# Threshold attention and a feed-forward part: one slot per head against one slot per pair of heads

## The chip, the cores and the metric

The kernel runs on one core of one Trainium2 chip. The metric is the device time of one execution in microseconds (us). Before the change the median of three runs is 1152.54 us (1152.47 to 1153.68).

## The reference

Eight batches of eight heads, 576 tokens, 64 dimensions a head, all float32. The attention keeps a key only where its score lies within tau of the row's maximum:

```python
scores = scale * np.matmul(q, k.transpose(0, 1, 3, 2))
thresh = np.max(scores, axis=-1, keepdims=True) - tau
scores = np.where(scores >= thresh, scores, -1000000000.0)
attn = np.exp(scores - np.max(scores, axis=-1, keepdims=True))
attn = attn / (np.sum(attn, axis=-1, keepdims=True) + 1e-09)
attn_out = np.matmul(attn, v)
```

Its output, the heads side by side as `x` (8 x 576 x 512), goes through a feed-forward part that mixes each token with the one before:

```python
xk = mu_k * x + (1.0 - mu_k) * x_prev
xr = mu_r * x + (1.0 - mu_r) * x_prev
k = np.maximum(xk @ w_k, 0.0)          # 512 -> 1024
v = k * k @ w_v                        # 1024 -> 512
r = 1.0 / (1.0 + np.exp(-(xr @ w_r)))
out = r * v
```

The weights arrive as float64 words.

## The kernel before, in words

**Jobs and slots.** A job is a batch and a pair of heads: 32 jobs. A job has nine slots, each one tile of 128 queries against all 576 keys: four tiles for each head, and one tile "T" that holds the last 64 queries of both heads. 288 slots in all.

**A slot's way through the engines.** `scores` (L297) multiplies on TensorE into two banks of PSUM (tile `s`, two buffers). `row_max` (L335, instruction L338) is on VectorE, `threshold` (L342) and `expo` (L344, L346) on ScalarE, `mask` (L348, L351) with its sum, `denom` (L355) and `inverse` (L358) on VectorE, `norm` (L360, L361) on GpSimd. `turn_p` (L364, L368) transposes the probabilities on TensorE into tile `pt` (one buffer). `p_hi` (L393) on ScalarE and `p_lo` (L403) on VectorE empty it as an upper and a lower float32r part, `attend` (L431, L439) multiplies both parts by the values, a head and up to 320 queries at a time, and `attend_out` (L447, L449) adds the two halves of the result into `xT` or `xE`. The stages of five neighbouring slots are in flight at once.

**Operands.** `load` (L151) brings a job's queries and keys with tokens on partitions. `prep_steps` (L182) transposes them on TensorE (L189, nine a job), splits them into upper and lower parts (L206 to L225) and stacks these by DMAs (`st`). Products are sums of float32r products of the parts. The first five jobs (`PLAIN`) multiply probabilities by values in float32 instead (`attend_tile`, L407, L412), and the first (`WHOLE`) its scores too (L308); the compiler turns each float32 product into two instructions.

**Weights.** 20 pieces of 128 x 512 are cut from float64 to float32 by one step on ScalarE, four on VectorE (clamp L132, then L136, L137, L138), then split (ScalarE, GpSimd), a piece every two slots from slot 4.

**Feed-forward part.** `ffn_chunk` makes 18 chunks of 256 tokens, each of 20 steps of TensorE (all at L525): eight of twelve matmuls of 256 columns (`h`), and four (`z`) and eight (`vps`) of six matmuls of 512 columns. A chunk's inputs are mixed by 18 steps on ScalarE and GpSimd (L485 to L510); for the first chunk these go one a slot until seven are left, and no feed-forward step runs before that.

**What sets the order.** `slot(n)` (L784) writes one slot's instructions. A credit (`TSLOT` less the planned time of the attention's matmuls) decides how many feed-forward steps a slot takes; ten steps are kept in hand until the end (`KEEP`). ScalarE runs in the order of the text (`manual_schedule`, which names ScalarE alone); on the other engines a scheduler orders the instructions by its own estimate.

Of the kernel before, what the change touches and what calls it, by code (L numbers as in the profile page):

```python
# [8 lines left out]
F32 = mybir.dt.float32  # L9
# [6 lines left out]
# float32 readings of the upper words of the doubles 2**-127 and just under 2**128  # L16
# [5 lines left out]
def tile_threshold_attention_then_rwkv_ffn(  # L22
    ctx: ExitStack,
    tc: tile.TileContext,
    q: bass.AP,
    k: bass.AP,
    v: bass.AP,
    tau: bass.AP,
    mu_k: bass.AP,
    mu_r: bass.AP,  # L30
# [8 lines left out]
    B, H, S, D = q.shape  # L39
    DM, DF = w_k.shape  # L40
    P = 128
    NPAIR = H // 2
    NCT = DM // P
# [3 lines left out]
    NC4 = SM // P  # L47
    HS = S // 2
    KT = S
    KM = S + ST  # L50
    W = 2 * S
# [25 lines left out]
    # The threshold uses max(tau, 0).  A negative tau masks every key, which leaves  # L77
    # equal scores, so the queries are scaled by zero then.
# [9 lines left out]
    # x^T of the first 512 tokens of a batch, behind a column of what comes before  # L88
    # them (zeros), and of the last 64 tokens, behind a copy of token 511.
# [7 lines left out]
    vraw = const.tile([P, 2, 5 * D], F32, name="vraw")  # L97

    # stationaries of the scores' tile that holds both heads' last 64 queries
# [3 lines left out]
    # The weights come as float64 words.  Each is cut to float32 (saturating, with what  # L103
    # lies under float32's normal range flushed to zero): the sign and the top bit of
    # the exponent stay, the three exponent bits under it repeat it in that range, and
    # the rest moves up by three bits.
    # A piece (128 rows, 512 columns) becomes its upper and lower part, where its words lay.
    pieces = {}

    def weight_jobs():  # L110
        jobs = []
        for nm, w in (("k", w_k), ("r", w_r), ("v", w_v)):
            for f in range(w.shape[1] // 512):
                for c in range(w.shape[0] // P):
                    src = w[c * P : (c + 1) * P, f * 512 : (f + 1) * 512]
                    jobs.append(((nm, c, f), src))
        return jobs

    def weight_steps(j, key, src):
# [3 lines left out]
        w1, w0 = words[:, :, 1], words[:, :, 0]  # L123
        box = {}

        def s1():
            box["t"] = xT[1][:, j % 4 if j < 16 else 1 + (j - 16) % 3, 1 : 1 + 512]
            A.activation(box["t"], w1.bitcast(F32), AF.Abs)

        def s2():  # L130
            t = box["t"]
            V.tensor_scalar(t, t, W_MIN, W_MAX, op0=ALU.max, op1=ALU.min)  # L132
# [18 lines left out]
    def load(job):  # L151
        b, hp = job["b"], job["hp"]
        hs = slice(2 * hp, 2 * hp + 2)
        raw = p1.tile([P, 9, 2, D], F32, tag="raw", name="raw")
        job["raw"] = raw
        for h in range(2):
            for g in range(2):
                SY.dma_start(
                    raw[:, 2 * g : 2 * g + 2, h],
                    q[b, 2 * hp + h, 2 * g * P : 2 * (g + 1) * P, :].rearrange("(p c) d -> p c d", c=2),  # L160
                )
            SY.dma_start(
                raw[:, 4:8, h], k[b, 2 * hp + h, 0:SM, :].rearrange("(p c) d -> p c d", c=NC4)
            )
        for s, src in ((0, q), (1, k)):
            SY.dma_start(
                raw[D * s : D * s + D, 8], src[b, hs, SM:S, :].rearrange("h s d -> s h d")
            )

    def load_v(job):  # L170
        b, hp = job["b"], job["hp"]
        hs = slice(2 * hp, 2 * hp + 2)
        SY.dma_start(
            vraw[:, :, 0 : 4 * D],
            v[b, hs, 0:SM, :].rearrange("h (p c) d -> p h (c d)", c=NC4),
        )
        for y in range(2):
            SY.dma_start(
                vraw[y * D : (y + 1) * D, :, 4 * D :], v[b, hs, SM:S, :].rearrange("h s d -> s h d")
            )  # L180

    def prep_steps(job):  # L182
        raw = job["raw"]
        box = {}

        def turn(nm, idx):
            ps = ps_w.tile([P, 512], F32, tag="w", name=nm)
            for j, i in enumerate(idx):
                PE.transpose(ps[:, j * P : (j + 1) * P], raw[:, i].rearrange("p h d -> p (h d)"), ident)  # L189
            box[nm] = ps  # L190

        def q_turn():
            if job["whole"]:
                job["qk"] = p3.tile([P, W], F32, tag="st1", name="qk")
                turn("pq", range(4))
                return
            box["hi"] = p1.tile([P, W], FR, tag="hi", name="hi")
            box["lo"] = p1.tile([P, W], FR, tag="lo", name="lo")
            turn("pq", range(4))

        def evac_q(cols, ps):
            if job["whole"]:
                A.activation(job["qk"][:, cols], ps, AF.Copy, scale=qscale)
                return
            hi, lo = box["hi"][:, cols], box["lo"][:, cols]
            A.activation(hi, ps, AF.Copy, scale=qscale)  # L206
            if ps.shape[1] == ST:
                tail = p2.tile([P, ST], F32, tag="tail", name="tail")
                A.activation(tail, ps, AF.Copy, scale=qscale)
                G.tensor_tensor(lo, tail, hi.bitcast(F32), op=ALU.subtract)  # L210
                return
            V.scalar_tensor_tensor(lo, ps, qscale, hi.bitcast(F32), op0=ALU.mult, op1=ALU.subtract)

        def evac_k(cols, ps):
            if job["whole"]:
                V.tensor_copy(job["qk"][:, cols], ps)
                return
            hi, lo = box["hi"][:, cols], box["lo"][:, cols]
            A.activation(hi, ps, AF.Copy)
            if ps.shape[1] == ST:  # L220
                tail = p2.tile([P, ST], F32, tag="tail", name="tail")
                A.activation(tail, ps, AF.Copy)
                G.tensor_tensor(lo, tail, hi.bitcast(F32), op=ALU.subtract)
                return
            V.tensor_tensor(lo, ps, hi.bitcast(F32), op=ALU.subtract)  # L225
# [758 lines left out]
```

## Time and profile before

| what | value |
|---|---|
| median of three runs | 1152.54 us |
| span of the profiled execution | 1151.2 us |
| its time by the three runs | 1152.47 to 1153.68 us, so 1.3 to 2.5 us lie around the span |
| PE busy, weight loads | 1104.4 us, 999.1 us |
| VectorE (DVE) busy | 961.3 us |
| ScalarE (ACT) busy | 846.0 us |
| GpSimd (POOL) busy | 673.3 us |
| DMA | 105.61 MB, 38.8% of the 16 engines' span |
| granted clock of TensorE | 1.00 in nearly every stretch |

In a row of a group stand the line, the engine, the operation, output and inputs, the count, then busy time and the mean of one in ns, then the idle time of the engine ahead of these instructions and what ended it. Matmul records overlap, since the array is pipelined; the distance between two starts is what a matmul costs in a row of them, and the duration holds some 0.17 us more until the result is out.

### The profile page before, as it was taken

What the parts mean: (1) busy time and instruction counts of PE and PEld (TensorE: products, weight loads), DVE (VectorE), ACT (ScalarE), POOL (GpSimd) and SP (SyncE); (2) the same over time, 40 slices, a digit from 0 to 9 for tenths busy, and PEclk for the clock granted to TensorE, in tenths of its full rate; (3) what the DMA queues carried; (4) which work ended last, traced back from release to release, by engine and by line L of the source; (5) the groups of instructions that cost most, each with busy time, mean ns of one, the idle gap of its engine ahead of it and who ended that gap; (6) DMA issues with size and microseconds to landing.
All of it is one profiled execution on the core that took longest, in us unless ns stands there. A gap on an engine that the chain in (4) does not pass through costs nothing.

```text
span 1151.2 us, 22514 instructions
## 1 busy us (share of the span) xinstructions
PE 1104.4 (96%) x7454; PEld 999.1 (87%) x7454; DVE 961.3 (84%) x2399; ACT 846.0 (73%) x1775; POOL 673.3 (58%) x860
## 2 busy tenths in 40 slices
PE   6999989999999999989999999999999999999998
PEld 4887878898989898988989898989898989898997
DVE  3899998888989898988989898989898989895222
ACT  3787877778687878768777878787878787876442
POOL 1465677465656465645747575656565656564672
PEclk9999999999999999999999999999999999999999
DMA  5777334433344344433334444423344444300000
GB/s 131 184 205 204 83 85 93 113 85 74 70 95 105 84 112 95 112 88 71 83 83 104 92 104 104 99 68 87 79 102 94 104 98 99 76 29 13 25 20 18
DMA packets 125027, 105.61 MB, mean 92 GB/s; under 512 B 93681, under 2 KB 101873, under 8 KB 124913
## 3 DMA queue, kind: packets, MB, share of 16 engines
q1 hardware_dynamic: 124912, 104.18, 38.8%
q8 instruction: 60, 0.98, 0.3%
q14 instruction: 55, 0.44, 0.1%
HBM read 39.85 MB, written 9.44 MB: 43 GB/s over the span
## 4 chain that ended last, share of the span: by engine, by line
PE 65%; DVE 18%; ACT 10%; issue 4%; SPq 1%; DMA 1%; POOL 1%; DVEq 0%; ACTq 0%; POOLq 0%
PE h L525 12%; PE vps L525 12%; PE pt L368 10%; PE s L326 9%; PE o L439 9%; PE z L525 8%; DVE p L351 4%; DVE sm L338 3%; DVE plo L403 2%; ACT phi L393 2%; ACT p L346 2%; DVE r L554 2%; PE o L412 1%; DVE phi L403 1%; DVE xT L137 1%
## 5 line engine op out<-in xcount | busy, mean ns | idle before, releaser
L361 POOL TENSOR_SCALAR p<-p,sm 128x576 f32<-128x576 f32 x288 | 222.6, 773 | 255.2 <-DVE sm L358 187.4
L393 ACT ACTIVATE phi<-pt 128x640 fp32r<-128x640 f32 (+1 forms) x270 | 172.4, 649 | 111.3 <-PE pt L368 110.6
L351 DVE SCALAR_TENSOR_TENSOR p<-s,sm,p 128x576 f32<-128x576 f32 x288 | 233.7, 811 | 23.4 <-ACT p L346 19.1
L338 DVE TENSOR_REDUCE sm<-s 128x1 f32<-128x576 f32 x288 | 215.9, 750 | 21.2 <-PE s L308 10.3
L525 PE MATMUL h<-xk,wk 128*128 128x256 f32 x1728 | 231.8, 285 | 1.0 <-ACT r L551 0.3
L525 PE MATMUL vps<-wv,k 128*128 128x512 f32 x864 | 227.2, 399 | 2.0 <-DVE sg L616 1.8
L368 PE MATMUL pt<-ident,p 128*128 128x128 f32 x1440 | 210.4, 276 | 18.6 <-DVE phi L403 8.9
L525 PEld LDWEIGHTS h<-xk,wk 128*128 128x128 f32 x1728 | 216.0, 191 | 4.1 <-ACT r L551 2.1
L346 ACT ACTIVATE p<-s,sm 128x576 f32<-128x576 f32 x288 | 212.6, 738 | 1.4
L368 PEld LDWEIGHTS pt<-ident,p 128*128 128x128 f32 x1440 | 168.2, 142 | 45.9 <-issue 13.5
L403 DVE TENSOR_TENSOR plo<-pt,phi 128x512 fp32r<-128x512 f32 (+1 forms) x270 | 170.5, 632 | 39.6 <-ACT phi L393 33.7
L525 PEld LDWEIGHTS vps<-wv,k 128*128 128x128 f32 x864 | 154.2, 188 | 29.1 <-DVE sg L616 2.9
L439 PE MATMUL o<-phi,vs 128*128 128x256 f32 (+1 forms) x540 | 156.1, 312 | 2.5 <-ACT phi L393 1.6
L439 PE MATMUL o<-plo,vs 128*128 128x256 f32 (+1 forms) x432 | 118.7, 296 | 0.2 <-DVE plo L403 0.2
L326 PE MATMUL s<-st 128*128 128x288 f32 x496 | 112.1, 308 | 5.0 <-DVE p L351 4.2
L558 POOL TENSOR_TENSOR k<-r,k 128x512 fp32r<-128x512 f32 x72 | 93.2, 1295 | 35.6 <-ACT k L557 35.1
L525 PE MATMUL z<-wr,xr 128*128 128x512 f32 x432 | 112.8, 400 | 0.1
L326 PE MATMUL s<-st,st 128*128 128x288 f32 x496 | 107.4, 298 | 0.1
L439 PEld LDWEIGHTS o<-phi,vs 128*128 128x128 f32 x540 | 101.8, 189 | 5.3 <-ACT phi L393 3.3
L342 ACT ACTIVATE sm<-sm,ntau 128x1 f32<-128x1 f32 x288 | 84.5, 293 | 20.8 <-DVE sm L338 19.1
L554 DVE TENSOR_TENSOR r<-r 128x512 f32<-128x512 f32 x72 | 76.8, 1066 | 27.0 <-ACT r L551 26.5
L326 PEld LDWEIGHTS s<-st 128*128 128x128 f32 x496 | 81.8, 191 | 17.4 <-DVE p L351 9.5
(91 smaller groups left out, 1792.5 us busy)
## 6 DMA issues: line engine op xcount, KB each, us to landing
st<-hi SPq DMA_DIRECT2D x62, 288.0 KB, 3.3
st<-lo SPq DMA_DIRECT2D x62, 288.0 KB, 4.1
st<-hi SPq DMA_DIRECT2D x62, 144.0 KB, 3.9
st<-lo SPq DMA_DIRECT2D x62, 144.0 KB, 4.2
raw<-in_q SPq DMA_DIRECT2D x128, 64.0 KB, 2.5
raw<-in_k SPq DMA_DIRECT2D x64, 128.0 KB, 2.9
vraw<-in_v SPq DMA_DIRECT2D x32, 256.0 KB, 2.8
out<-sg SPq DMA_DIRECT2D x32, 256.0 KB, 2.4
```

Of the source, the lines that this page charges most:

```text
L326: PE.matmul(s[:, y, 0:HS], l, r[:, KT + y * HS : KT + (y + 1) * HS], start=(j == 0), stop=(j == n - 1),)
L338: V.tensor_reduce(x["sm"][0], x["s"], axis=AX.XY, op=ALU.max, negate=True)
L346: A.activation(x["p"].rearrange("p (a b) -> p a b", a=2), x["s"], AF.Exp, bias=x["sm"][0])
L351: V.scalar_tensor_tensor(pv, x["s"], thr, pv, op0=ALU.is_ge, op1=ALU.mult, accum_out=sums)
L361: G.tensor_scalar(x["p"], x["p"], x["sm"][3], 0.0, op0=ALU.mult, op1=ALU.add)
L368: PE.transpose(x["pt"][:, c, :], x["p"][:, o : o + P], ident)
L393: A.activation(hi[:, :, off : off + sl.stop - sl.start], x["pt"][:, :, sl], AF.Copy)
L403: V.tensor_tensor(d, x["pt"][0:n, y, sl], hi[0:n, y, cs].bitcast(F32), op=ALU.subtract)
L439: PE.matmul(o[:, 0:n], l, r, start=(j == 0), stop=(j == len(prods) - 1))
L525: PE.matmul(ps, l, r, start=(x == 0), stop=(x == len(prods) - 1))
L554: V.tensor_tensor(r, r, r, op=ALU.mult)
L558: G.tensor_tensor(k2[:, 1, js], r, k2[:, 0, js].bitcast(F32), op=ALU.subtract)
```

## The change

- **Layout.** The host arranges the inputs: queries (with scale left out) and keys come transposed, one head's last 64 keys ahead of all its keys (`qk`); values come as pairs with zeros beside the last 64 keys; the mixing factors and the weights' words in the order in which they are read. No transposes of inputs and no stacking DMAs remain. `x` holds one head's operands, on both halves of the partitions, in one buffer.
- **Slots.** A slot is 128 queries of both heads of a pair: scores in two tiles `s` (the two buffers), nine transposes in three groups of three, each in a bank of its own (`pt`, two buffers), emptied by ScalarE, VectorE, ScalarE. A job has four such slots and one with the last 64 queries of both heads. Batch 0 is done in two passes, first two slots of each pair of heads, then the three others.
- **Values.** Probabilities stay float32 and are copied once. `attend` multiplies in float32, head 0 into partitions 0 to 63 of the output and head 1 into 64 to 127, so each product uses one half of the array's columns. No lower parts and no sum of halves.
- **Other moves.** Thresholds go from ScalarE to VectorE, the weights' clamp from VectorE to GpSimd; two pieces of weights start in every slot from slot 1.
- **Order.** All four engines run in the order of the text.

The core of it:

```diff
-    TSLOT, TSTEP, KEEP, N0 = 3.325, 1.3, 10, 36
-    PLAIN, WHOLE = 5, 1
+    TPAIR, TLAST, TSTEP, KEEP = 6.85, 3.43, 1.385, 10
...
-    ps_t = ctx.enter_context(tc.tile_pool(name="ps_t", bufs=1, space=bass.MemoryType.PSUM))
+    ps_t = ctx.enter_context(tc.tile_pool(name="ps_t", bufs=2, space=bass.MemoryType.PSUM))
...
-    ctx.enter_context(tc.manual_schedule(engines={A.engine}))
+    ctx.enter_context(tc.manual_schedule(engines={A.engine, PE.engine, V.engine, G.engine}))
...
+    def load(job, h):
+        b, hp = job["b"], job["hp"]
+        x = p1.tile([P, W], F32, tag="x", name="x")
+        for y in range(2):
+            SY.dma_start(x[y * D : (y + 1) * D], qk[b, 2 * hp + h])
+        job["x"] = x
...
+    def prep(job, h):
...
+        A.activation(qh, x[:, 0:SM], AF.Copy, scale=qscale)
+        A.activation(kx, x[:, S:W], AF.Copy)
+        A.activation(th, x[:, SM:S], AF.Copy, scale=qscale)
+        V.scalar_tensor_tensor(
+            ql, x[:, 0:SM], qscale, qh.bitcast(F32), op0=ALU.mult, op1=ALU.subtract
+        )
+        G.tensor_tensor(kx[D:P], x[D:P, S:W], kx[D:P].bitcast(F32), op=ALU.subtract)
+        V.scalar_tensor_tensor(
+            tl, x[:, SM:S], qscale, th.bitcast(F32), op0=ALU.mult, op1=ALU.subtract
+        )
...
+    def turn(x, g):
...
+        ps = ps_t.tile([P, 512], F32, tag="pt", name="pt")
...
+        for j, i in enumerate(range(3 * g, 3 * g + 3)):
+            m = blocks[i].shape[1]
+            PE.transpose(ps[0:m, j * P : (j + 1) * P], blocks[i], ident)
+        x["pt", g] = ps
...
+    def attend(job, g):
+        n = 256 + g * ST
+        pT, vt = job["pT"][g], job["v"]
+        o = ps_w.tile([P, 512], F32, tag="w", name="o")
+        for c in range(5):
+            for h in range(2):
+                hs = slice(h * D, (h + 1) * D)
+                i = 4 if c == 4 else 5 * h + c
+                PE.matmul(o[hs, 0:n], vt[:, c, hs], pT[:, i], start=(c == 0), stop=(c == 4))
+        return o
...
+        if x is not None:
+            scores(x)
+        flush_a()
+        if x is not None:
+            row_max(x)
+            threshold(x)
+        av(0)
+        one_step()
+        if x1 is not None:
+            turn(x1, 0)
+            turn(x1, 1)
+        if x is not None:
+            expo(x, 0)
+        if x1 is not None:
+            evac(x1, 0, A)
+        if x is not None and x["n"] > 1:
+            expo(x, 1)
+        if x1 is not None:
+            evac(x1, 1, V)
+            if x1["t"] != "T":
+                turn(x1, 2)
+                evac(x1, 2, A)
+        av(1)
+        if x is not None:
+            mask(x)
+            inverse(x)
+            norm(x)
+        rest()
+        one_step()
...
+        while state["credit"] > 0 and micro(keep):
+            state["credit"] -= TSTEP
```

TensorE in the middle of the program, before: `s` are scores, `h` a feed-forward step, `pt` transposed probabilities, `o` a head's values (the last matmul of a group).

```order
L439 MATMUL o_8117<-phi_8025,vs_0_7720 128x256
L326 MATMUL s_8161<-st1_0_7656 128x288 x2
L326 MATMUL s_8161<-st1_0_7656,st2_0_7657 128x288 x2
L525 MATMUL h_8074<-xk_7737,wk00_446 128x256 x3
L525 MATMUL h_8074<-xk_7737,wk10_524 128x256 x3
L525 MATMUL h_8074<-xk_7737,wk20_612 128x256 x3
L525 MATMUL h_8074<-xk_7737,wk30_698 128x256 x3
L368 MATMUL pt_8180<-ident_81,p_8037 128x128 x5
```

TensorE in the middle of the program, now: the slot in which both groups of values (`o`) are multiplied, and the start of the slot of last queries (`bd`).

```order
L197 MATMUL s_4880<-kx_4615,qh_4613 128x288 x2
L197 MATMUL s_4880<-kx_4615,ql_4614 128x288 x2
L197 MATMUL s_4885<-kx_4615,qh_4613 128x288 x2
L197 MATMUL s_4885<-kx_4615,ql_4614 128x288 x2
L305 MATMUL o_4896<-pT0_4535,v_4261 64x256 x10
L270 MATMUL pt_4908<-ident_81,p_4824 128x128 x3
L270 MATMUL pt_4912<-ident_81,p_4824 128x128 x3
L270 MATMUL pt_4921<-ident_81,p_4824 128x128 x3
L305 MATMUL o_4926<-pT1_4665,v_4261 64x320 x10
L197 MATMUL s_4946<-kx_4615,bd_98 128x288 x8
L379 MATMUL vps_4871<-wv20_862,k2_4465 128x512 x3
```

Scores of two heads stand together, values of both heads form one group, transposes come in threes, and in this slot no feed-forward step stands between them.

ScalarE in the middle of the program, before: `ot` is the copy of half of a head's values, `p` the exponential, `phi` the copy out of `pt`, `hi` a split of keys, `sm` a threshold, `xk` a mixing step.

```order
L447 ACTIVATE ot_7941<-o_7925 64x320
L342 ACTIVATE sm_7945<-sm_7945,ntau_88 128x1
L346 ACTIVATE p_7948<-s_7901,sm_7945 128x576
L277 ACTIVATE vs_1_7950<-vraw_98 128x5x64
L507 ACTIVATE xk_7737<-mk_7850 128x512
L393 ACTIVATE phi_7836<-pt_7968 128x5x128
L219 ACTIVATE hi_7880<-pk_7981 128x512
```

ScalarE now, from a mixing step (`mk`) to the copies of the values; `pT0` and `pT1` are the transposed probabilities of the two groups.

```order
L351 ACTIVATE mk_4838<-m_4801,mu_sb_92 128x256 x2
L225 ACTIVATE p_4824<-s_4813,sm_4823 128x576
L275 ACTIVATE pT1_4665<-pt_4841 128x3x128
L225 ACTIVATE p_4824<-s_4818,sm_4823 128x576
L275 ACTIVATE pT1_4665<-pt_4853 128x3x128
L440 ACTIVATE sg_4790<-z_4830 128x512
L361 ACTIVATE xk_4837<-mk_4838 128x512
L310 ACTIVATE xT1_95<-o_4896 128x256
L225 ACTIVATE p_4891<-s_4880,sm_4890 128x576
L275 ACTIVATE pT0_4917<-pt_4908 128x3x128
```

The thresholds are gone from ScalarE; the mixing step stands ahead of a slot's first exponential, and the copy of the values (L310) ahead of the exponential of its slot.

More of the change, by code (lines that the diff above doesn't have):

```diff
@@ L112, in weight_jobs @@
         for nm, w in (("k", w_k), ("r", w_r), ("v", w_v)):
[L113 to L116, printed above, removed]
+            for f in range(w.shape[1]):
+                for c in range(w.shape[0]):
+                    jobs.append(((nm, c, f), w[c, f]))
         return jobs
@@ L370, in group @@
-    def group(job, h, g):
-        if (h, g) not in job["groups"]:
-            job["groups"][(h, g)] = (
-                p2.tile([P, 5, 320], FR, tag="phi", name="phi"),
-                p2.tile([P, 4, 320], FR, tag="plo", name="plo"),
-            )
-        return job["groups"][(h, g)]
-    def dests(x):
-        job, t = x["job"], x["t"]
-        if t[0] == "T":
-            return [
-                (group(job, h, job["tg"]), 2 * P, slice(h * ST, (h + 1) * ST)) for h in range(2)
-            ]
-        h, c = t
-        return [(group(job, h, c // 2), (c % 2) * P, slice(0, P))]
@@ new lines, in threshold, with halves, expo, mask @@
+    def threshold(x):
+        sm = x["sm"]
+        for u in range(x["n"]):
+            V.tensor_scalar(
+                sm[:, 2 + u : 3 + u], sm[:, u : u + 1], -1.0, ntau, op0=ALU.mult, op1=ALU.add
+            )
+    def halves(ap):
+        return ap.rearrange("p (a b) -> p a b", a=2)
+    def expo(x, u):
+        A.activation(halves(x["p"][:, u]), x["s"][u], AF.Exp, bias=x["sm"][:, u : u + 1])
+    def mask(x):
+        sm = x["sm"]
+        for u in range(x["n"]):
+            pv = halves(x["p"][:, u])
+            V.scalar_tensor_tensor(
+                pv,
+                x["s"][u],
+                sm[:, 2 + u : 3 + u],
+                pv,
+                op0=ALU.is_ge,
+                op1=ALU.mult,
+                accum_out=sm[:, 4 + u : 5 + u],
+            )
@@ new lines, in inverse, with norm, group @@
+    def inverse(x):
+        sm, n = x["sm"], x["n"]
+        V.tensor_scalar(sm[:, 4 : 4 + n], sm[:, 4 : 4 + n], 1e-9, None, op0=ALU.add)
+        V.reciprocal(sm[:, 6 : 6 + n], sm[:, 4 : 4 + n])
+    def norm(x):
+        for u in range(x["n"]):
+            p = x["p"][:, u]
+            G.tensor_scalar(p, p, x["sm"][:, 6 + u : 7 + u], 0.0, op0=ALU.mult, op1=ALU.add)
+    def group(job, g):
+        if g not in job["pT"]:
+            job["pT"][g] = p1.tile([P, 9, 256 + g * ST], F32, tag=f"pT{g}", name=f"pT{g}")
+        return job["pT"][g]
@@ L656, in tile_threshold_attention_then_rwkv_ffn @@
-    av_at = {}
-    for (ji, h, g), n in last_slot.items():
-        if not jobs[ji]["plain"]:
-            av_at.setdefault(n + 4, []).append((ji, h, g))
-    ready = {}
-    def when(sel):
-        return max(n for (ji, h, g), n in last_slot.items() if sel(jobs[ji], g)) + 4
+        job["last"] = len(slots) - 1
+    av_at, ready, edge_at = {}, {}, {}
+    for ji, job in enumerate(jobs):
+        n = job["due"] = job["last"] + 2
+        av_at[n] = [(job, g) for g in job["groups"]]
     for b in range(B):
@@ L680, in tile_threshold_attention_then_rwkv_ffn @@
+    prep_at = {}
+    for ji, job in enumerate(jobs[:-1]):
+        off = {2: 0, 3: 1, 5: 2}[len(job["tiles"])]
+        for h in range(2):
+            prep_at[job["start"] + off + h] = (ji + 1, h)
     wjobs = weight_jobs()
@@ L874, in weights @@
+        if chunks and chunks[0]["first"]:
+            if len(chunks[0]["mix"]) > 7:
+                chunks[0]["mix"].pop(0)()
+        for c in ready.get(n, []):
+            chunks.append(ffn_chunk(*c))
+        while state["credit"] > 0 and micro(keep):
+            state["credit"] -= TSTEP
+        state["credit"] = min(state["credit"], 0.0)
+        for _ in range(2):
             for w in list(wq):
```

629 lines of the change are left out of this document (163 added, 466 removed).

## Prediction

> **What bounds the kernel now.** I read the page first, then the same execution cut into its three stages, then single rows. The page's busy line, its slices and the chain that ended last:
>
> ```profile
> span 1151.2 us, 22514 instructions
> PE 1104.4 (96%) x7454; PEld 999.1 (87%) x7454; DVE 961.3 (84%) x2399; ACT 846.0 (73%) x1775; POOL 673.3 (58%) x860
> ...
> DVE  3899998888989898988989898989898989895222
> ...
> PE 65%; DVE 18%; ACT 10%; issue 4%; SPq 1%; DMA 1%; POOL 1%; DVEq 0%; ACTq 0%; POOLq 0%
> ```
>
> TensorE leads the chain and VectorE is second; DMA is nowhere, so the loads that the change removes are worth nothing by themselves. Busy time of all engines in three stretches (start to first feed-forward matmul, to the last attention, to the end), and of the feed-forward matmuls of L525 alone:
>
> ```profile
> 12.60:160.30 147.70, 134.99 (x880) 114.43 (x879) 130.57 (x308) 111.70 (x255) 80.64 (x105) 0.98 0.64 164
> 160.30:1046.30 886.00, 863.99 (x5973) 792.36 (x5972) 803.85 (x2050) 688.63 (x1441) 535.52 (x687) 1.00 0.39 88
> 1046.30:1151.20 104.90, 100.35 (x592) 89.09 (x590) 25.21 (x37) 43.35 (x78) 55.52 (x61) 1.00 0.07 21
> ...
> 160.30:1046.30 886.00, 473.39 (x2467) 362.87 (x2468) 1.00 0.39 88
> ```
>
> Columns are length, then busy us and count of PE, PEld, DVE, ACT, POOL, and the clock. Up to 160.3 us no feed-forward matmul runs: five jobs of attention go by. The middle holds the other 27 jobs and 2467 feed-forward matmuls, the end the rest of them. Busy PE overstates, since its records overlap; starts are needed. Some of them, from the timeline (start, duration, instruction, count):
>
> ```profile
> 599.94 0.30 PE L439 MATMUL o<-plo,vs 128*128 128x320 f32 x1
> ...
> 600.66 0.31 PE L439 MATMUL o<-phi,vs 128*128 128x320 f32 x1
> 600.81 0.43 PE L326 MATMUL s<-st 128*128 128x288 f32 x2
> 601.08 0.42 PE L326 MATMUL s<-st,st 128*128 128x288 f32 x2
> 601.34 1.54 PE L525 MATMUL vps<-wv,k 128*128 128x512 f32 x6
> 602.72 0.71 PE L368 MATMUL pt<-ident,p 128*128 128x128 f32 x5
> 603.26 0.27 PE L189 MATMUL pt<-ident,raw 128*128 128x128 f32 x1
> ...
> 606.77 0.28 PE L439 MATMUL o<-plo,vs 128*128 128x256 f32 x1
> ...
> 607.61 0.28 PE L439 MATMUL o<-phi,vs 128*128 128x256 f32 x1
> 608.26 1.60 PE L525 MATMUL h<-xk,wk 128*128 128x256 f32 x12
> 609.70 0.71 PE L368 MATMUL pt<-ident,p 128*128 128x128 f32 x5
> ```
>
> From start to start: four score matmuls 0.53; five transposes 0.54, so 0.109 each; values 0.12 (256 columns, seven steps in 0.84) and 0.144 (320 columns, five in 0.72); a feed-forward step 1.44 (twelve of 256 columns) or 1.38 (six of 512). A job of attention is 40 score matmuls (5.3), 54 transposes (5.9), 18 value matmuls of each width (4.75): 15.9 us. A chunk is 8 steps of 1.44 and 12 of 1.36 to 1.38: 27.8. The middle is then 27 x 15.9 = 429 plus 2467/168 = 14.7 chunks = 408, together 837 of 886 us. TensorE loses 49 us there, 1.8 a job. The start is VectorE's, the middle TensorE's at 94.5%, the end pure TensorE.
>
> **The change, part by part.** Sums are made against the span, 1151.2; the median of the three runs lies 1.3 above it.
>
> *TensorE's own work.* Scores and feed-forward steps stay. Nine transposes of inputs a job go, and three of probabilities (42 remain, 4.6). Values are now float32. Their price is read at the first job, which multiplies in float32:
>
> ```profile
> 30.43 1.62 PE L308 MATMUL s<-qk 64*64 64x288 f32 x8
> ...
> 33.89 1.13 PE L308 MATMUL s<-qk 64*128 64x288 f32 x4
> 34.95 0.77 PE L368 MATMUL pt<-ident,p 128*128 128x128 f32 x5
> ...
> L308 PE MATMUL s<-qk x8: 402/497/737, 30.4 to 31.6; 64*64 64x288 f32 x8
> ```
>
> Each float32 product shows as two instructions (the code asks for half as many). Four that use the same rows take (1.13 - 0.40)/3 = 0.243 a step for 288 columns, so an estimate of 0.216 for 256 and 0.27 for 320. Eight on two quarters of the array start within 1.2 us, where one after another would need 7 x 0.243 = 1.7: they run in pairs. If the two halves of the columns pair likewise, the 20 instructions of a group count as 10: 2.16 and 2.70, plus 0.1 for each of four changes of shape (33.89 + 4 x 0.243 = 34.86, and the next shape starts at 34.95): 5.3 a job. TensorEngine Tiling (Array Packing) in the Trainium skill, Tiling Modes, says that tiles of the array execute in parallel, 128x64 among them; the trace shows quarters on rows of their own, and no run shows halves that share rows. A job is then 5.3 + 4.6 + 5.2 = 15.1, 0.8 less.
>
> *The start.* The order shows the first feed-forward step in slot 20 (chunk 0 is ready at slot 9, and its mixing lets one step go a slot, eleven of them): after four jobs, not five. What sets the time of those slots is VectorE:
>
> ```profile
> L351 DVE SCALAR_TENSOR_TENSOR p<-s,sm,p 128x576 f32<-128x576 f32 x288 | 233.7, 811 | 23.4 <-ACT p L346 19.1
> L338 DVE TENSOR_REDUCE sm<-s 128x1 f32<-128x576 f32 x288 | 215.9, 750 | 21.2 <-PE s L308 10.3 <-PE s L326 8.9
> L554 DVE TENSOR_TENSOR r<-r 128x512 f32<-128x512 f32 x72 | 76.8, 1066 | 27.0 <-ACT r L551 26.5
> L403 DVE TENSOR_TENSOR plo<-pt,phi 128x256 fp32r<-128x256 f32 x54 | 22.8, 422 | 4.2 <-PE s L326 2.4 <-ACT phi L393 0.9
> L216 DVE COPY qk<-pk 128x512 f32<-128x512 f32 x1 | 0.7, 692 | 4.8 <-PE pk L189 4.8
> L355 DVE TENSOR_SCALAR sm<-sm 128x1 f32<-128x1 f32 x288 | 41.8, 145 | 2.0
> L136 DVE TENSOR_SCALAR xT<-xT 128x512 uint32<-128x512 uint32 x20 | 12.8, 638 | 0.0
> ...
> 44.62 0.14 DVE L355 TENSOR_SCALAR sm<-sm 128x1 f32<-128x1 f32 x1
> 44.68 0.42 DVE L132 TENSOR_SCALAR xT<-xT 128x512 f32<-128x512 f32 x1
> ```
>
> A pair slot: two maxima 1.50, two masks with their sums 1.79, two thresholds 0.29 (new on VectorE, off ScalarE), two small steps 0.30, one copy of 384 columns 0.56 (between the 0.42 and 0.69 rows): 4.4. A slot of last queries: 2.9. Lower parts of queries read two operands from SBUF, so between the 0.69 and 1.07 rows: I take 1.07 as GpSimd is busy, plus 0.2 for the tail, 16 times: 20. Weights keep three steps, some 2.6 a piece (L136 0.64, two like the 1.07 row): 52; their clamp goes to GpSimd, which has room (80.64 of 147.7). In all 16 x 4.4 + 4 x 2.9 + 20 + 52 = 154. Neighbours overlap by 0.08 (the last two rows), some 300 times: 130 busy. At the 88% of the row of the start that is 148, at 98% it is 133; I take 140, and 12 ahead of it, as now (x has one buffer, so head 1 loads only after head 0 is split). TensorE's first step then comes at 152 (145 to 162), with 28 jobs to go, one more than before.
>
> *The waits of an order by hand.* TensorE now takes its instructions strictly as written, so whatever a transpose waits for holds the feed-forward step behind it. In a pair slot the third group of transposes needs a buffer that ScalarE or VectorE must first empty:
>
> ```profile
> L346 ACT ACTIVATE p<-s,sm 128x576 f32<-128x576 f32 x288 | 212.6, 738 | 1.4
> L393 ACT ACTIVATE phi<-pt 128x640 fp32r<-128x640 f32 x216 | 151.8, 703 | 100.7 <-PE pt L368 100.0
> L393 ACT ACTIVATE phi<-pt 128x320 fp32r<-128x320 f32 x54 | 20.6, 435 | 10.6 <-PE pt L368 10.6
> ```
>
> Counted from the slot's start: scores to 1.05, a step to 2.44, six transposes to 3.1; the first three are out of the array at 2.9, ScalarE copies 384 columns in 0.49 (between 0.435 and 0.703), and the seventh starts at 3.5. That is 0.4 lost, three times a job. In the slot where both groups of values are multiplied no step stands ahead, ScalarE waits for the first values before its exponential, and the loss is 0.75. After the slot of last queries the next scores wait for its mask: maximum to 2.0, exponential to 2.8, copy to 3.8, mask to 4.6, where TensorE is at 4.35: 0.35 with the hops. Where input splits stand ahead of the maximum on VectorE, exponential and copy come 0.2 to 0.8 later; I add 0.2 once. In all 2.5 a job, against 1.8 now: 70 over 28 jobs. Below, the bound is one 0.4 alone with the rest hidden; above, see the third rival.
>
> *Slots without steps.* By the order nine slots after slot 20 run out of feed-forward steps (in the second half of batch 1, and at the turns to batches 2, 3 and 4). A pair slot then lasts as long as its chain, 0.7 + 0.75 + 0.7 + 0.3 + 0.56 + 1.7 + 0.2 = 4.9, where TensorE has 2.0: six times 2.7, and 2 for the short slots: 18.
>
> ScalarE sheds the thresholds and half of the evacuation, GpSimd gains splits and has room; both cost nothing as long as TensorE leads, and are priced in the third rival.
>
> **The sum.** 152 + 28 x 15.1 (423) + 18 x 27.8 (501) + 70 + 18 + 8 (the last row of the stages, 104.9, less 559/168 chunks, 92.5, and the last values) = 1172, and 1.3 to the median: **1173 us**, 1.8% slower. The saving of 0.8 a job (26) is eaten by a start that is only 8 shorter for one job less (33), and by waits.
>
> **The rivals.** *The waits hide (faster).* If the buffer for the third group comes free in time, because VectorE's copy ends before ScalarE's and the mask chain stays under a slot, the loss is about 1.0 a job: 1173 - 28 x 1.5 = 1131. It decides from 1.8 lost a job down, (1173 - 1152)/28 below mine. For it: VectorE falls from 30 busy us a job (803.85/27) to some 22 (4 x 4.4 + 2.9 + 2 x 1.3 + 3 for the feed-forward part, less 0.08 for each of 60). Against it: copy after transposes takes longer than three transposes, whatever else is idle.
>
> *ScalarE held by GpSimd.* The row of GpSimd's scaling:
>
> ```profile
> L361 POOL TENSOR_SCALAR p<-p,sm 128x576 f32<-128x576 f32 x288 | 222.6, 773 | 255.2 <-DVE sm L358 187.4 <-PE s L326 39.3 <-PE o L439 16.6
> ```
>
> ScalarE's order puts mixing steps ahead of the exponential, and they wait for GpSimd, where two scalings of 0.77 stand first. One such wait of 1.5 a job makes 1173 + 42 = 1215. The row speaks for it only in part: GpSimd now idles 255 us ahead of this group, waiting for VectorE.
>
> *The halves do not overlap* (the change doesn't do what it says): 4.9 more a job, 32 x 4.9 = 156, so 1329; with an overlap of half, 1251. TensorE: Matmul & The Clock Gate in the Trainium skill, Measured speedup vs the span model, gives 2.38 times for three column tiles; an estimate of 1.6 for two would make 4.9 into 1.25 a job and the time 1213.
>
> **How the numbers follow.** Forecast 0.37 (1150 to 1200), waits hidden 0.35 (1090 to 1150), ScalarE held 0.16 (1200 to 1235), halves apart 0.12. The range 1105 to 1235 leaves out most of the last and the tail of the second. About 0.2% is what a measurement can tell here, 2.3 us. Faster 0.35, almost all from the second case; same 0.05, where forecast and second case meet; slower 0.60, the rest. Slower alone reaches from 1155 to 1235.
>
> **What would show it.** Right: first feed-forward matmul near 152 us; float32 value matmuls on half the columns starting in pairs, a group of ten products in 2.3 and 2.8 us; transposes of a third group with 0.4 idle ahead of them on ScalarE's copy; a job of 32 to 33 us from slot 21 on. Wrong: value groups of 4.3 us or more; a first step before 140; or PE idle under 1 us a job in the middle.

## The result, and the profile after

The changed kernel takes 1480.47 us (1479.65 to 1483.03), the kernel before 1152.51 (the median of four runs): a ratio of 1.287 (1.283 to 1.290). The direction was forecast, the size was not: 1480 lies far above the range of 1105 to 1235. The page of the changed kernel, first its busy line, then the slices of TensorE, VectorE and the granted clock, then the chain:

```profile
span 1478.8 us, 19592 instructions
PE 1144.4 (77%) x6928; PEld 917.1 (62%) x6928; DVE 902.8 (61%) x2013; ACT 743.1 (50%) x1436; POOL 748.0 (51%) x702
...
PE   2533445888687888788878797988888888889998
...
DVE  4787655656765557476756566556666666666211
...
PEclk9656656999799999999999999999999999999999
...
PE 44%; DVE 15%; ACT 14%; POOL 12%; DMA 10%; issue 4%; SPq 1%; POOLq 0%; ACTq 0%; DVEq 0%
```

Over the whole span no engine is busy for more than 77%; TensorE's share of the chain falls from 65 to 44%. The three stages (to the first feed-forward matmul, to the last row maximum, to the end), then the feed-forward matmuls of the middle alone, columns as before:

```profile
11.10:252.90 241.80, 106.79 (x475) 77.18 (x476) 165.84 (x310) 97.24 (x190) 133.40 (x98) 0.65 0.33 94
252.90:1365.30 1112.40, 930.23 (x5827) 747.41 (x5825) 709.91 (x1665) 596.28 (x1159) 550.69 (x531) 0.95 0.17 45
1365.30:1478.80 113.50, 107.34 (x628) 92.45 (x628) 24.12 (x33) 46.69 (x85) 61.71 (x67) 0.99 0.06 19
...
252.90:1365.30 1112.40, 473.03 (x2448) 385.76 (x2448) 0.95 0.17 45
```

With the prediction's own prices for TensorE's work (15.1 a job, 27.8 a chunk of 168 matmuls) the forecast's terms stand against these rows so:

| term | forecast | measured |
|---|---|---|
| first feed-forward step | 152 | 252.9 |
| middle beyond 28 jobs (423) and 2448/168 = 14.6 chunks (405) | 70 + 18 = 88 | 1112.4 - 828 = 284 |
| end beyond 576/168 = 3.4 chunks (95.3) | 8 | 18 |

The differences, 101, 196 and 10, are the 307 us between 1173 and 1480. So the question is what delays the start by 100 and each job by 7. What TensorE waits for (us in total, times, longest), over the whole span:

```profile
PE pt L270 <- ACT pT L275: 117.1, 70, 10.0
PE s L197 <- DVE p L231: 67.3, 48, 7.4
PE s L197 <- POOL kx L176: 55.0, 10, 11.1
PE pt L270 <- DVE pT L277: 54.1, 50, 6.4
```

The third transposes wait for copies on ScalarE and VectorE, scores wait for masks and for the lower keys of GpSimd. All ten waits for lower keys lie in the start; in the middle 104.9 us (63.2 and 41.7) are waits for copies and 43.3 for masks. Why copies and masks are late there shows in the timeline of one job (start, duration, engine, instruction; in brackets the wait):

```profile
714.41 0.42 PE L197 MATMUL s<-kx,ql 128*128 128x288 f32 x2
...
714.54 0.75 POOL L249 TENSOR_SCALAR p<-p,sm 128x576 f32<-128x576 f32 x1 [2.77 <-DVE sm L244]
714.63 1.20 DVE L173 SCALAR_TENSOR_TENSOR ql<-x,qscale,qh 128x512 fp32r<-128x512 f32 x1 [0.26 <-ACT qh L170]
...
715.38 1.87 POOL L176 TENSOR_TENSOR kx<-x,kx 64x640 fp32r<-64x640 f32 x1
715.75 1.58 DVE L177 SCALAR_TENSOR_TENSOR bd<-x,qscale,bd 128x64 fp32r<-128x64 f32 x1
...
717.25 1.41 DVE L212 TENSOR_REDUCE sm<-s 128x1 f32<-128x576 f32 x2
...
718.03 0.74 ACT L225 ACTIVATE p<-s,sm 128x576 f32<-128x576 f32 x1 [2.09 <-DVE sm L212]
...
721.51 0.50 PE L197 MATMUL s<-kx,qh 128*128 128x288 f32 x2 [1.77 <-DVE p L231]
...
722.42 0.72 ACT L170 ACTIVATE qh<-x,qscale 128x512 fp32r<-128x512 f32 x1 [1.65 <-DMA x<-in_qk]
...
728.25 0.55 PE L270 MATMUL pt<-ident,p 128*128 128x128 f32 x3 [1.58 <-ACT pT L275]
```

The slot's last scores are out at 714.8, but VectorE stands in two input splits until 717.3; maximum, exponential, mask and next scores follow over 2 us late, one behind the other. The split of only 64 columns (L177) takes 1.58 us and ends with GpSimd's subtraction (715.38 + 1.87).

The waits have a second effect, in TensorE's clock. The same job has one feed-forward step twice, first at the full clock and then, after the wait of 1.77 us, at a lower one; below the two steps stand all engines' busy time in the two stretches and the clock, columns as before:

```profile
718.20 1.55 PE L379 MATMUL z<-wr,xr 128*128 128x512 f32 x6
...
722.86 2.58 PE L379 MATMUL z<-wr,xr 128*128 128x512 f32 x6
```

```profile
718.20:719.70 1.50, 1.50 (x8) 0.94 (x6) 1.50 (x5) 1.50 (x4) 0.42 (x1) 1.00 0.66 169
722.90:725.40 2.50, 2.50 (x8) 1.86 (x8) 2.14 (x3) 1.59 (x4) 2.50 (x3) 0.53 0.03 7
```

At a clock of 0.53 the step takes 2.58 us instead of 1.55. The middle had a mean clock of 1.00 before and has 0.95 now; 5% of its 1112 us is some 56 us, an estimate of the most that the lower clock can have added to TensorE's work there: about 2 of the 7 us a job.

The groups, of the changed kernel and then of the kernel before:

```profile
L177 DVE SCALAR_TENSOR_TENSOR bd<-x,qscale,bd 128x64 fp32r<-128x64 f32 x72 | 77.7, 1079 | 3.9
L173 DVE SCALAR_TENSOR_TENSOR ql<-x,qscale,qh 128x512 fp32r<-128x512 f32 x72 | 66.6, 925 | 58.2 <-ACT qh L170 57.5
L176 POOL TENSOR_TENSOR kx<-x,kx 64x640 fp32r<-64x640 f32 x72 | 124.0, 1723 | 33.4 <-ACT kx L171 27.5 <-POOL p L249 0.7 <-POOL mk L358 0.2
L128 POOL TENSOR_SCALAR xT<-xT 128x512 f32<-128x512 f32 x20 | 40.2, 2013 | 0.2
```

```profile
L212 DVE SCALAR_TENSOR_TENSOR lo<-pq,qscale,hi x31: 732/750/754, 23.2 to 985.9; 128x512 fp32r<-128x512 f32 x31
...
L225 DVE TENSOR_TENSOR lo<-pk,hi x31: 669/692/693, 27.7 to 993.2; 128x512 fp32r<-128x512 f32 x31
...
L210 POOL TENSOR_TENSOR lo<-tail,hi x31: 316/324/771, 23.7 to 999.9; 128x64 fp32r<-128x64 f32 x31
```

Before, one split served both heads of a job (its two heads lie on the two halves of the partitions): 1.44 us of VectorE and 2 x 0.32 of GpSimd a job (a row like the last stands for the keys' tail). Now each head lies on both halves and is split by itself: 2 x (0.93 + 1.08) = 4.0 of VectorE and 2 x 1.72 = 3.4 of GpSimd. The prediction gave this work its price in the start; in the middle it put GpSimd's part at nothing, since TensorE would lead there, and VectorE's at 0.2 a job.

### The profile page after: what moved, and what is told of

It is laid out like the page before. It is cut to its first block, busy times and chain, and to the rows that moved or that the text cites. A ratio compares the mean times of both kernels' runs of the same rounds, so it can differ in the third digit from the quotient of the medians.

```text
span 1478.8 us, 19592 instructions
## 1 busy us (share of the span) xinstructions
PE 1144.4 (77%) x6928; PEld 917.1 (62%) x6928; DVE 902.8 (61%) x2013; ACT 743.1 (50%) x1436; POOL 748.0 (51%) x702
## 4 chain that ended last, share of the span: by engine, by line
PE 44%; DVE 15%; ACT 14%; POOL 12%; DMA 10%; issue 4%; SPq 1%; POOLq 0%; ACTq 0%; DVEq 0%
PE o L305 11%; PE h L379 10%; DMA x<-in_qk 10%; PE vps L379 7%; PE pt L270 7%; PE s L197 6%; DVE bd L177 4%; PE z L379 3%; POOL p L249 3%; POOL kx L176 3%; ACT p L225 3%; ACT qh L170 3%; ACT pT L275 3%; DVE ql L173 2%; DVE p L231 2%
## 5 line engine op out<-in xcount | busy, mean ns | idle before, releaser
L270 PE MATMUL pt<-ident,p 128*128 128x128 f32 (+1 forms) x1344 | 229.8, 304 | 174.3 <-ACT pT L275 117.1
L270 PEld LDWEIGHTS pt<-ident,p 128*128 128x128 f32 (+1 forms) x1344 | 166.6, 153 | 236.3 <-ACT pT L275 137.9
L225 ACT ACTIVATE p<-s,sm 128x576 f32<-128x576 f32 x288 | 213.5, 741 | 166.1 <-DVE sm L212 161.5
L197 PE MATMUL s<-kx,qh 128*128 128x288 f32 x512 | 133.8, 346 | 105.0 <-DVE p L231 66.5
L277 DVE COPY pT<-pt 128x384 f32<-128x384 f32 (+3 forms) x224 | 96.8, 432 | 138.0 <-PE pt L270 105.6
L275 ACT ACTIVATE pT<-pt 128x384 f32<-128x384 f32 (+3 forms) x352 | 149.8, 427 | 55.2 <-PE pt L270 44.9
L305 PE MATMUL o<-pT,v 128*64 128x320 f32 (+1 forms) x1280 | 174.4, 420 | 0.0
L197 PEld LDWEIGHTS s<-kx,qh 128*128 128x128 f32 x512 | 90.3, 211 | 134.2 <-issue 65.1
L176 POOL TENSOR_TENSOR kx<-x,kx 64x640 fp32r<-64x640 f32 x72 | 124.0, 1723 | 33.4 <-ACT kx L171 27.5
L305 PEld LDWEIGHTS o<-pT,v 128*64 128x64 f32 x1280 | 88.4, 141 | 65.2 <-issue 16.1
L197 PE MATMUL s<-kx,ql 128*128 128x288 f32 x512 | 120.7, 321 | 0.0
L310 ACT ACTIVATE xT<-o 128x256 f32<-128x256 f32 x64 | 24.6, 384 | 170.5 <-PE o L305 170.5
```

Of the source, the lines that this page charges most:

```text
L176: G.tensor_tensor(kx[D:P], x[D:P, S:W], kx[D:P].bitcast(F32), op=ALU.subtract)
L197: PE.matmul(s[:, y, 0:HS], l, job["kx"][:, h, o + y * HS : o + (y + 1) * HS], start=(j == 0), stop=(j == len(prods) - 1),)
L225: A.activation(halves(x["p"][:, u]), x["s"][u], AF.Exp, bias=x["sm"][:, u : u + 1])
L270: PE.transpose(ps[0:m, j * P : (j + 1) * P], blocks[i], ident)
L275: A.activation(d, s, AF.Copy)
L277: e.tensor_copy(d, s)
```

## The experiments

Single runs, each beside a run of the kernel before on the same chip (1148.7 to 1153.6, a spread of 0.4%); differences under some 7 us (an estimate from that spread) tell nothing. "Start" is the first feed-forward matmul (252.9 above), "a job" the time from there to the last row maximum by 28 (39.7 above).

**The order of the text.** Four kernels change the list of engines that run in the order of the text. e_sched, as in the kernel before only ScalarE:

```diff
-    ctx.enter_context(tc.manual_schedule(engines={A.engine, PE.engine, V.engine, G.engine}))
+    ctx.enter_context(tc.manual_schedule(engines={A.engine}))
```

> The changed kernel with the order of the text kept for ScalarE alone, as before; a scheduler orders TensorE, VectorE and GpSimd. Theory of the order (what stands late in one queue holds the next slot's work behind it): the middle falls from 41.4 us a job to 36 or less, and the time from 1480 to under 1340. Theory of the work (float32 values, splits out of SBUF and new copies cost the time, in whatever order): it stays within 3%, over 1435.

Measured 1345.57 (start 208, a job 36.4): the order costs 135 of the 307. Then the scheduler on TensorE alone (`engines={A.engine, V.engine, G.engine}`) and on VectorE and GpSimd alone (`engines={A.engine, PE.engine}`):

> The changed kernel with a scheduler's order on TensorE alone; ScalarE, VectorE and GpSimd stay in the order of the text. The scheduler on all three gave 1346, the text on all 1480. Theory that TensorE's own queue is the loss (feed-forward steps stand behind transposes and scores that wait): 1350 to 1390. Theory that VectorE's and GpSimd's queues are (they hold the next maximum, and with it all that TensorE waits for): over 1440.

> The counterpart: a scheduler's order on VectorE and GpSimd, the order of the text on TensorE and ScalarE. Theory of VectorE's queue: 1350 to 1390. Theory of TensorE's queue: over 1440. If both matter, each alone gives about half, 1400 to 1430.

1402.31 and 1362.99: 78 and 117, which overlap. More of the price goes through VectorE's and GpSimd's queues than through TensorE's, on which the prediction had put it. The converse, the kernel before with all four engines in the order of its text:

```diff
-    ctx.enter_context(tc.manual_schedule(engines={A.engine}))
+    ctx.enter_context(tc.manual_schedule(engines={A.engine, PE.engine, V.engine, G.engine}))
```

> The kernel before with all four engines in the order of its text, nothing else changed. Theory of the order: it loses too, since its text was written for a scheduler: 1210 to 1350. Rival (its stages lie four slots apart, so the text's order has slack and only the pair slots' short pipeline suffers): within 3%, under 1185.

1519.48, 366 above the 1153.55 beside it. So the order of the text is no price of the new layout alone; the old text, which was written for a scheduler, pays more for it.

**One suspected wait at a time.** The clamp of the weights (e_clamp, L128), and the lower keys (e_kx, L176), each back on VectorE by one letter:

```diff
-            G.tensor_scalar(t, t, W_MIN, W_MAX, op0=ALU.max, op1=ALU.min)
+            V.tensor_scalar(t, t, W_MIN, W_MAX, op0=ALU.max, op1=ALU.min)
...
-        G.tensor_tensor(kx[D:P], x[D:P, S:W], kx[D:P].bitcast(F32), op=ALU.subtract)
+        V.tensor_tensor(kx[D:P], x[D:P, S:W], kx[D:P].bitcast(F32), op=ALU.subtract)
```

> The weights' clamp back on VectorE (0.47 us there before the change, 2.01 on GpSimd after it). Theory of the order: the two engines pass each weight to and fro at the end of a slot, ahead of the next maximum, so the start shortens by 20 x 2 = 40 us to about 1440, the middle unchanged. Theory of VectorE as the bound of the start: it has 9 us more to do, so the start stays or grows by 9.

> The lower part of the keys (64 x 640) moves from GpSimd to VectorE. Theory of contention (VectorE's two splits out of SBUF take 0.93 and 1.08 us because GpSimd works at 1.72 us beside them): both fall to 0.75 and 0.2, the new one takes 0.85, the next maximum comes 1 us earlier twice a job, and the time falls by 30 to 60 us. Rival (VectorE is late because it waits for ScalarE's parts, and more work on it makes it later): same, or slower by 28 x 1 us.

1466.04 (start 239) and 1475.43 (start 230, a job 40.4). The clamp costs 14, all in the start. Moving the keys changes nothing in the sum: it saves 23 in the start and gives it back in the jobs, where VectorE has 1.2 us a head more (87.3 us in 72), of which its small split gives back 0.44 (1.08 to 0.64). e_turn puts the third transposes and their copy behind the second group of values, `norm` and a feed-forward step:

```diff
-            if x1["t"] != "T":
-                turn(x1, 2)
-                evac(x1, 2, A)
...
+        if x1 is not None and x1["t"] != "T":
+            turn(x1, 2)
+            evac(x1, 2, A)
```

> The third group of transposes goes behind the values and a feed-forward step, so that its buffer is empty when TensorE comes to it. Theory that this wait is the loss (137 us of TensorE's idle time in the middle ends with a copy out of that buffer): 1480 falls to about 1350. Theory of the late chain (the copy is late because the exponential ahead of it is): TensorE waits next for the masks, and no more than 40 us are gained, 1440.

1418.34, 62 less with the start unchanged: 2.2 a job. The prediction had 1.95 for these transposes (0.4 three times, 0.75 in the slot where both groups of values are multiplied), so this term was about right. The two theories ahead of the run, 1350 and 1440, both missed. e_x2 gives the inputs two buffers and loads a head one ahead (the tile `p` gets two buffers instead of three, for room):

```diff
-        x = p1.tile([P, W], F32, tag="x", name="x")
+        x = p2.tile([P, W], F32, tag="x", name="x")
...
-        x["p"] = p3.tile([P, 2, S], F32, tag="p", name="p")
+        x["p"] = p3.tile([P, 2, S], F32, tag="p", name="p", bufs=2)
...
-                load(jobs[ji], 1)
...
-            elif ji + 1 < len(jobs):
-                load(jobs[ji + 1], 0)
+            if ji + 1 < len(jobs):
+                load(jobs[ji + 1], h)
```

> Two buffers for one head's operands (x), each loaded a head earlier, as the changed kernel otherwise; for room the probabilities have two buffers and not three. Theory of the load (ScalarE waits 76 us for x to arrive, with the next exponential behind it, and the next job's scores wait for keys 55 us): the start shortens by 20 to 30 us and the middle by 1 to 2 us a job, to 1400 to 1430. Rival (ScalarE would only wait for something else): within 15 us of 1480.

1435.92, 44 less (start 235): the wait of ScalarE for the inputs, 76.3 us in the changed kernel, was partly on the path. All four edits together, in the order of the text (e_all):

> Four single edits together, still all in the order of the text: clamp on VectorE, lower keys on VectorE, third transposes behind values and a step, two buffers for x. If their waits are independent, the gains add (14, 5, 62 and that of x): about 1360 to 1380. If each wait hid another, more than the sum: under 1330. If one takes the other's place: over 1390.

1383.96: 96 less, which is under the sum of the four (126): in part, where one wait goes, another takes its place.

**The splits.** e_nosplit leaves out the lower parts of queries and keys, and with them the exactness of the scores: VectorE's two instructions and GpSimd's one a head go, and the scores multiply the upper part in their place, so that TensorE's work stays.

```diff
-            job["ql"] = p2.tile([P, 2, SM], FR, tag="ql", name="ql")
+            job["ql"] = job["qh"]
...
-        V.scalar_tensor_tensor(
-            ql, x[:, 0:SM], qscale, qh.bitcast(F32), op0=ALU.mult, op1=ALU.subtract
-        )
-        G.tensor_tensor(kx[D:P], x[D:P, S:W], kx[D:P].bitcast(F32), op=ALU.subtract)
-        V.scalar_tensor_tensor(
-            tl, x[:, SM:S], qscale, th.bitcast(F32), op0=ALU.mult, op1=ALU.subtract
-        )
```

> The changed kernel without the lower parts of queries and keys: the two splits on VectorE and the one on GpSimd are left out, and the upper part of the queries stands in for the lower. TensorE's work is the same. Theory of the splits (two of VectorE's instructions a head, slowed by GpSimd, stand ahead of the next maximum, and the scores wait for GpSimd's part): 3 us or more a job and 30 in the start, 1480 to about 1360. Rival (the wait is for x and for ScalarE's parts, or for the third transposes): under 1.5 a job, over 1420.

1338.06: 142 less, 39 in the start and 3.7 a job, about as much as the order's 135; the prediction had 0.2 a job for their place ahead of the maximum. Is it the place or the work? e_late issues VectorE's two behind the next slot's maximum and threshold, in jobs of five slots (`prep` returns them as a function):

```diff
             row_max(x)
             threshold(x)
+        if "late" in state:
+            state.pop("late")()
```

> The changed kernel with the two splits of queries and keys on VectorE issued behind the maximum and threshold of the next slot, in jobs of five slots; all work is done. Theory, they cost by their position ahead of the maximum: 1370 to 1410, the job falls from 39.7 to 37 us or less. Rival, they cost by their work, and by the inputs and GpSimd that they wait for, wherever they stand: 1450 to 1485, the job stays above 39.

1475.45: nothing to speak of. TensorE's waits for masks fall (67.3 to 47.0), those for VectorE's copies rise (54.1 to 80.4), and ScalarE's wait for inputs, which are now held longer, rises from 76.3 to 127.0. The last could hide a gain, so e_x2_late repeats it with two input buffers:

> Two buffers for the inputs (as in e_x2, 1436) and, besides, the two splits on VectorE behind the maximum and threshold of the next slot. The splits set late hold the inputs longer, and with one buffer the rounding of the next queries then waits for its load (127 us of ScalarE in e_late, 76 in the changed kernel); with two this excuse is gone. Theory, position ahead of the maximum, masked in e_late by the inputs: 1370 to 1400. Rival, the work itself, which only meets another wait (the copy of the transposes): 1425 to 1445.

1412.65, 23 below e_x2: between the two expectations. The place is worth 0.8 a job (23 us) once the inputs don't mask it, a third of the 69 us that the two splits turn out to cost in the next run; the rest is put down to the work itself. Whose work, show e_noql (VectorE's two left out) and e_nokx (GpSimd's subtraction left out):

> Only the two splits on VectorE are left out (72 of 0.93 and 72 of 1.08 us, 144 in all; the lower queries are taken from the upper, so the scores are less exact); the subtraction of the keys on GpSimd stays. Theory, the work of VectorE is what costs: 1360 to 1390, most of the 142 us that leaving out all three gave. Rival, GpSimd's subtraction and what waits for it cost: 1430 to 1470.

> Only the subtraction of the keys on GpSimd is left out (72 of 1.72 us; the lower keys are then the upper, so the scores are wrong by a factor); the two splits on VectorE stay. Theory, the work of VectorE costs, GpSimd matters by slowing it (VectorE's small split 1.08 beside GpSimd, some 0.3 without): 1410 to 1440. Rival, the subtraction and what waits for it cost: 1350 to 1390.

1411.89 and 1409.74: 69 and 71, together 139, near the 142 of e_nosplit. My theory, that VectorE's work was nearly all of it, falls; half is GpSimd's. VectorE's two cost in the jobs (start 247, a job 37.5), GpSimd's one in both (start 228, a job 38.1). One way in which GpSimd's costs shows in VectorE's small split, in e_nokx (the first row) and in the changed kernel:

```profile
L176 DVE SCALAR_TENSOR_TENSOR bd<-x,qscale,bd 128x64 fp32r<-128x64 f32 x72 | 46.8, 650 | 3.3
```

```profile
L177 DVE SCALAR_TENSOR_TENSOR bd<-x,qscale,bd x72: 499/1094/1593, 9.6 to 1326.2; 128x64 fp32r<-128x64 f32 x72
```

That is 31 us of VectorE; the scores' wait for keys falls too (55.0 to 26.6, now for ScalarE's). How the 71 divide between the two is open. e_nocut leaves out the clamp and the three steps of VectorE that make float32 of the weights' words, so the weights are other numbers:

```diff
-            G.tensor_scalar(t, t, W_MIN, W_MAX, op0=ALU.max, op1=ALU.min)
...
-            V.tensor_scalar(u, u, 0x07FFFFFF, 3, op0=ALU.bitwise_and, op1=ALU.logical_shift_left)
-            V.scalar_tensor_tensor(u, w1, 0xC0000000, u, op0=ALU.bitwise_and, op1=ALU.bitwise_or)
-            V.scalar_tensor_tensor(u, w0, 29, u, op0=ALU.logical_shift_right, op1=ALU.bitwise_or)
```

> The changed kernel without the cutting of the weights to float32: the clamp on GpSimd and the three steps on VectorE are left out, the loads, copies and splits stay. Theory that the start is long because the two engines pass the weights to and fro ahead of each slot's maximum: more than VectorE's own time for them (59 us in this profile) goes, the first feed-forward step comes 70 us or more earlier, at about 180, and the time is about 1410. Theory that the start is long because each job's operands come just in time: under 40 us go, over 1440.

1431.76 (start 204, a job 39.7): 49 less, all in the start; 52 of VectorE's busy time was forecast for it.

**Do the terms add up?** e_all_sched has the scheduler on three engines, clamp and lower keys on VectorE and two input buffers; e_vg_all all four edits of e_all, with the scheduler on VectorE and GpSimd alone:

> The changed kernel with the scheduler's order on TensorE, VectorE and GpSimd, clamp and lower keys on VectorE, two buffers for x. Theory of the order plus single waits: under 1300, as the order alone gave 1346 and the other edits shorten the start by 30 or more. Theory that the scheduler already hid them: 1330 to 1346.

> The order of the text is kept on TensorE and ScalarE, and the scheduler places the work of VectorE and GpSimd; besides, the clamp of the weights and the lower keys are on VectorE, the third group of transposes stands last, and the inputs have two buffers. Theory, the order costs through the queues of VectorE and GpSimd, and the waits that the four edits take away are others: 1240 (1225 to 1265), below the 1279 of the kernel in which the scheduler places the work of TensorE too, since the value groups keep their pairs (2.4 and 2.9 us). Rival, the order of TensorE is also a cost: 1275 to 1330.

1278.90 and 1251.42. The second is the best form of the changed kernel that was found, 229 us below it and 103 above the kernel before beside it; no form that computes the reference's result beat the kernel before. The two differ in the place of the third transposes too, but one price of the scheduler on TensorE shows: it breaks groups of values apart. In e_all_sched 24 of the 64 groups stand whole, in e_vg_all all of them. The matmuls of one group in e_all_sched and in e_vg_all:

```profile
511.17 1.29 PE L305 MATMUL o<-pT,v 128*64 128x320 f32 x6
512.87 2.37 PE L305 MATMUL o<-pT,v 128*64 128x320 f32 x14
```

```profile
506.21 2.91 PE L305 MATMUL o<-pT,v 128*64 128x320 f32 x20
```

Last, e_nosplit_sched: e_all_sched without the lower parts, as in e_nosplit.

> The lower parts of queries and keys are left out (so the scores are less exact), the scheduler places the work of three engines, the clamp is on VectorE and the inputs have two buffers. Theory, splits, order and waits are the whole distance between forecast and result: 1160 to 1200, near the forecast of 1173. Rival, something else is missing in the sum (a start that stays above 170 us, jobs above 33 us): over 1220.

1182.53. Its stages:

```profile
11.00:153.70 142.70, 98.36 (x436) 64.86 (x437) 117.85 (x271) 84.17 (x167) 63.17 (x57) 0.75 0.57 160
153.70:1066.00 912.30, 889.93 (x5845) 712.41 (x5844) 613.81 (x1581) 598.40 (x1180) 447.75 (x482) 0.99 0.21 56
1066.00:1180.80 114.80, 109.74 (x647) 95.22 (x645) 24.66 (x32) 46.87 (x86) 61.90 (x66) 1.00 0.06 19
```

The start is 153.7 (forecast 152), the middle loses 912.3 - 423 - 2438/168 x 27.8 (403) = 86 (forecast 88). With the order, the splits and the waits for clamp and inputs gone, 298 of the 307 us are gone, so these together are the distance. That the forecast's own sum comes out is in part luck, and no proof of its terms: the forecast held the splits' 20 us in the start and an order by hand, which this kernel does not.

## Why the prediction was wrong

- **TensorE's own work: right, at the full clock.** Halves of the columns do pair. Both groups of one job in the changed kernel:

```profile
702.10 2.38 PE L305 MATMUL o<-pT,v 128*64 128x256 f32 x20
...
706.41 2.91 PE L305 MATMUL o<-pT,v 128*64 128x320 f32 x20
```

  Ten pairs of 0.216 and 0.27 were forecast, 2.16 and 2.70, and some 0.2 until the last is out. TensorEngine Tiling (Array Packing) in the Trainium skill, Tiling Modes, had it so; the row now agrees for halves that share rows. That rival is dead.
- **The start: wrong by 101.** "At the 88% of the row of the start that is 148, at 98% it is 133; I take 140." VectorE's work was 166 us, not 130, and filled 69% of the time. Of the 36, 10 are the splits (17 of each kind, 13.2 and 16.9, where 20 stood), 9 the weights' three steps (61.3 in the rows of the start, 52 forecast) and some 12 overlap: the durations in this stretch add up to about 178, so neighbours overlap by 12 and not by 24. Some 5 stay without a name. The 69% is the failed step: 88 to 98% was taken over from a kernel whose VectorE a scheduler keeps filled, for one in which it waits in the order of the text. What VectorE waits for in the start:

```profile
DVE xT L132 <- POOL xT L128: 26.5, 9, 4.0
DVE ql L173 <- ACT qh L170: 22.3, 7, 6.1
DVE pT L277 <- ACT pT L275: 11.8, 10, 4.6
DVE sm L212 <- PE s L197: 9.2, 9, 3.7
```

  These are the clamp, ScalarE's upper queries (ScalarE itself waits 23.8 us there for the inputs), ScalarE's copies and the scores, which in turn wait 55.0 us for GpSimd's lower keys. Where the scheduler places VectorE's work, and clamp and lower keys are VectorE's too (e_vg_all), VectorE fills 165.4 of the 185.0 us of the start, 89%. By the experiments, weights' steps 49, scheduler 45, splits 39, lower keys 23, two input buffers 18, clamp 14; these overlap.
- **GpSimd "has room" for the clamp: wrong.** It has, but the clamp takes 2.01 there instead of 0.47 on VectorE (the mean of the kernel before; 0.91 when moved back, in e_clamp), and VectorE waits 26.5 us for it where the prediction had no wait.
- **The waits, 2.5 a job: far too small.** With the slots without steps 3.1 a job were forecast, and 10.1 came. The places were named (third transposes, scores behind the mask), the sizes came from slots in which VectorE and ScalarE are punctual. "Where input splits stand ahead of the maximum ... I add 0.2 once" is the term that failed most: leaving the splits out gives 3.7 a job. The price of the third transposes held (1.95, and 2.2 in e_turn). The prediction had no term for the order on VectorE's and GpSimd's queues (117 us in e_vg, start and jobs together), nor for TensorE's lower clock.
- **"Both cost nothing as long as TensorE leads": TensorE no longer leads.** It is 84% busy in the middle, 97.5% before. The sentence is about ScalarE and GpSimd. GpSimd's splits rise from 0.6 to 3.4 us a job (and VectorE's from 1.4 to 4.0), and leaving out GpSimd's alone gives 71 us. The sums of work don't show this: in the middle VectorE's busy time falls from 29.8 us a job (803.85/27) to 25.4 (709.91/28), and GpSimd's stays (19.8 and 19.7). What grew, by the timeline of the job above, is the chain from one slot's scores to the next slot's, in which the splits now stand. They are not all of it: without them a job still takes 36.0.
- **ScalarE held by GpSimd:** that wait is there. ScalarE's mixing steps wait 63.5 us for GpSimd (34.4, 15.4 and 13.7, in 39 times), more than the 42 of the rival, though less than the 161.5 in which its exponentials wait for VectorE's maxima. What these waits add to the time stays open, since no run takes them away alone. *The waits hide:* no.
- **The end: right** within 10 us.

## What to carry to other kernels

Before work is put down as hidden by the leading engine, follow one item's chain through all queues with that work in it. The busy time of each engine for one round isn't enough: here it fell or stayed on VectorE and GpSimd, and the chain still grew. With a fixed order a late step on one queue makes the next queue's step late too. A layout in which one instruction serves a head, where it had served a pair, needs twice as many of them, on whichever engine they run. A share of busy time belongs to the order in which it was measured, and isn't carried over to another order.

## What the runs showed of the hardware

- VectorE's step with two inputs from SBUF takes 0.50 to 1.59 us for the same 64 columns, on average 1.08; without GpSimd's subtraction the average is 0.65. In the timeline it ends with that subtraction. SBUF — State Buffer in the Trainium skill, SBUF: two separate sides, calls the pair of ports that VectorE and GpSimd share an exclusive lock, which the first to start holds for its whole instruction (on VectorE's side, among others, one with two inputs from SBUF against a GpSimd instruction that reads SBUF). The rows at 715.38 and 715.75 agree.
- GpSimd's clamp (maximum and minimum, 128 x 512) takes 2.01 us, its multiplication by a column (128 x 576) 0.85; the clamp had been 0.47 on VectorE.
- The granted clock is lower where TensorE idles more: 0.65 in the start, where it is 44% busy, 0.95 in the middle at 84%, 0.99 at the end at 95%. A step of six matmuls took 1.55 us at 1.00 and 2.58 at 0.53. How much of this lies on the path that sets the time no run separates.
